# Convolution and gated MLP on one core: the second product sums its row halves in two banks side by side

## The chip, the cores and the metric

The kernel runs on one core of a Trainium2 chip. The metric is the device time of one execution in microseconds (us). Three runs of the kernel before took 718.79, 719.27 and 721.37 us; the median, 719.27, is what the change is measured against.

A core has five queues that run by themselves and wait for each other through semaphores: TensorE (PE, matmuls; its weight loads are listed apart as PEld), VectorE (DVE), ScalarE (ACT), GpSimd (POOL) and SyncE (SP), which computes nothing and issues transfers. Each works through its own instructions in the order in which the program gives them.

## The reference

The input x has 8 sequences of 4096 tokens with 192 channels in float32. There are two stages.

1. A causal convolution over 7 tokens. The channels fall into 8 heads of 24; each head has its own 7 weights, put through a softmax first: `out[b,s,h,:] = sum_k softmax(weight)[h,k] * x[b, s+k-6, h, :]`, with zeros ahead of the sequence.
2. A gated MLP on each of the 32768 tokens: `h = x @ w_in` (192 to 2048), `g = h * cos(h)`, `out = g @ w_out` (2048 to 192).

The kernel's matmuls take bf16 operands and sum in float32.

## The kernel before

**Tiles and units.** A tile (index t) is 512 tokens, and there are 64. A unit (index u) is two tiles: loading, casting, convolution and transposing go by units, both products by tiles. The main loop runs 66 times, since work on a tile trails its first product by up to two passes. A pass with even t is the first of its unit, one with odd t the second (`second`).

**Way of the data.** SP loads a unit of x; POOL casts it to bf16. PE convolves it by matmuls against a banded matrix (`conv_mm`), ACT copies the sums into ct (`conv_out`), and POOL doubles it (`double_unit`). SP then issues one transposing transfer for the unit (`turn_unit`), so that the channels come to lie on the partitions in cT, and POOL mends a few columns of it (`mend_edges`). Product 1 (`mm1`) multiplies cT with w_in in eight groups per tile. Each group fills two PSUM banks of h. For each, ACT makes cos(h) as a sine with an offset, and DVE multiplies h by it, which gives g (`gcu`). Product 2 (`mm2_step`) multiplies g with w_out into o_ps; a copy brings o_ps to SBUF (`evac`), and SP stores it (`store`).

**Row halves.** Nearly all matmuls use half of PE's rows: the upper 64 and the lower 64 work as two arrays at once, so matmuls come in pairs (r = 0 and r = 1). Each half sums over its part of the contraction, and both sums must end in the same bank. [...] They therefore take turns on two banks, and at each change of turns the half that comes to a bank waits until the other has left it. The class `Turn` does this through a no-op on SP's queue: `mark` makes the no-op wait for the last matmul of one half, and `wait` makes the first matmul of the other half wait for the no-op. Convolution parts take a turn in the same manner: c1 is the half of a part ahead of its turn, c2 the half after it.

**Product 2 before.** Work is cut into phases of 32 steps. In phase n the upper rows sum into one bank, and the lower rows sum into the bank that the upper rows filled in phase n - 1. So the two banks of a tile (b = 0 and 1, each for 256 of its tokens) come ready one phase apart, ACT copies both out, and there are 129 phases, of which the first and the last have one half only.

**PSUM.** Six of the eight banks are a ring of three buffers (`h_pool`), which product 1 and the convolution share; the other two hold o_ps.

**The orders.** Nothing is scheduled by a tool: strings give the order of the work on PE and ACT. In `PE_ORDER` (line 400, steady) h0 to h7 are the groups of product 1, c1 and c2 the convolution, m7 means seven steps of product 2 (a pair of matmuls each), and p and q mark places where a phase has ended. `ACT_ORDER` has s0 to s7 for the cosines (DVE's products go with them), ec1 and ec2 for the copies of the convolution, P and Q for the copies of o_ps. `PE_FIRST` and `ACT_FIRST` hold the first four passes. The transfers are tied to p and q: `turn_unit` for the next unit is issued at q of even passes, loads at p of odd passes, stores at p. SP's queue so holds loads, transposes, stores and the no-ops of the turns, in that order in which the loop writes them.

Of the kernel before, what the change touches and what calls it, by code (L numbers as in the profile page):

```python
# [8 lines left out]
FP32 = mybir.dt.float32  # L9
# [7 lines left out]
def kernel(  # L17
# [8 lines left out]
    nc = tc.nc  # L26
    B, S, D = x.shape
# [4 lines left out]
    T = 512  # L32
    NT = NTOK // T
    NB = T // 128
    U = 1024
    NU = NTOK // U
# [35 lines left out]
    def load_unit(u, n0=0, n1=UB, queue=nc.sync):  # L72
        if n0 == 0:
            x_tiles[u] = xin.tile([128, UB + 1, D], FP32, name="x_f")
        queue.dma_start(out=x_tiles[u][:, n0:n1, :],
                          in_=xf[u * U + n0 * 128 : u * U + n1 * 128, :].rearrange("(n p) d -> p n d", p=128))
# [119 lines left out]
    def conv_out(u, c, ps, n0, m0, m1, copy, double=False, banks=(0, 1)):  # L196

        for b in banks:
            w0 = (2 * c + b) * 2 * R
            o = ct_tiles[u][:, m0:m1, :, :, w0 : w0 + 2 * R].rearrange("p n k t w -> p (n k) t w")  # L200
            i = ps[b][:, (m0 - n0) * 2 * G : (m1 - n0) * 2 * G].rearrange("p (m t w) -> p m t w", t=1, w=2 * R)
            if double:
                copy(o, i.to_broadcast([128, (m1 - m0) * NC, 2, 2 * R]))  # L203
            else:
                copy(o[:, :, 0, :], i[:, :, 0, :])  # L205

    def ring_banks():
        h = h_pool.tile([128, 2, T], FP32, name="h")
        return [h[:, 0, :], h[:, 1, :]]
# [39 lines left out]
    def turn_unit(u, n0=0, n1=UB + 1):  # L249
        ct = ct_tiles.pop(u)  # L250
        if u not in cT:
            cT[u] = cT_pool.tile([128, UB + 1, NC, 128], BF16, name="cT")
        nc.sync.dma_start_transpose(out=cT[u][:, n0:n1].rearrange("p n c k -> p (n c) k"),
                                    in_=ct[:, n0:n1].rearrange("p n c t k -> p (n c t k)"))
        cT.pop(u - 2, None)
# [62 lines left out]
    def conv_rest():  # L318
        banks = o_banks()
        for c in range(2):  # L320
            for i in range(4):
                for prev in range(2):
                    conv_mm(0, c, [b[:, 4 * G * 2 * c :] for b in banks], i, slice(0, 128), NB + 1 - prev, UB + 1 - prev, prev,
                            start=c == 0 and prev == 0 and i % 2 == 0, stop=c == 1 and prev == 1 and i % 2 == 1)
        for b in range(2):
            for c in range(2):
                conv_out(0, c, [x[:, 4 * G * 2 * c :] for x in banks], NB, NB, UB, copies[1 - b], True, (b,))

    conv_first()
    turn_first(0)  # L330
# [31 lines left out]
    STEPS = 2 * NF  # L362

    def mm2_step(q):
        phase, i = divmod(q, STEPS)
        f, si = divmod(i, 2)
        for r in range(2):
            tt, b = divmod(phase - r, 2)
            if not 0 <= tt < NT:
                continue  # L370
            if r == 0 and i == 0:

                last = (tt, b) == (NT - 1, 1)
                o_ps[tt, b] = ring_banks()[0] if last else o_pools[b].tile([128, T], FP32, name="o_ps%d" % b)
            rows = slice(64 * r, 64 * r + 64)
            s = 2 * b + si
            m = nc.tensor.matmul(out=o_ps[tt, b][:, si * D : (si + 1) * D],  # L377
                                 lhsT=g_tiles[tt][rows, f, s * 128 : (s + 1) * 128], rhs=wo[rows, f // 2, f % 2, :],
                                 start=(r == 0 and i == 0), stop=(r == 1 and i == STEPS - 1), skip_group_check=True)
            if r == 0 and i == STEPS - 1:  # L380
                turns[tt, b] = Turn()
                turns[tt, b].mark(m)
            if r == 1 and i == 0:
                turns.pop((tt, b)).wait(m)

    def evac(t, b):
        if b == 0:
            o_sb[t] = opool.tile([128, NB, D], FP32, name="o_sb")
        nc.scalar.copy(o_sb[t][:, 2 * b : 2 * b + 2, :].rearrange("p s d -> p (s d)"), o_ps.pop((t, b))[:, 0 : 2 * D])  # L389

    def store(t, b0=0, b1=2):
        nc.sync.dma_start(out=out[t * T + b0 * 256 : t * T + b1 * 256, :].rearrange("(n p) d -> p n d", p=128),
                          in_=o_sb[t][:, 2 * b0 : 2 * b1, :])

    o_ps, o_sb, turns = {}, {}, {}
# [1 line left out]

    PE_ORDER = "h0 m7 c1 m6 c2 m4 h1 m7 q h2 h3 m12 h4 m10 h5 m10 h6 h7 p m8"  # L400
    ACT_ORDER = "s0 ec1 ec2 s1 Q s2 s3 s4 s5 P s6 s7"

    PE_FIRST = ["h0a h0b h1 h2 r h3 h4 h5 d1 d2 h6 h7 c1 c2 p",
                "m8 h0 m2 h1 m11 h2 m7 h3 m4 q h4 m9 d1 d2 m7 h5 m7 h6 m1 c1 c2 m8 p h7",
                "m9 c1 m1 h0 m6 c2 m9 h1 m7 q h2 h3 m15 h4 m5 h5 m12 p h6 h7",
                "m8 c1 m6 c2 m5 h0 m9 h1 m3 h2 m1 q h3 m14 h4 m7 h5 m11 h6 h7 p m8"]
    ACT_FIRST = ["s0a s0b s1 s2 s3 s4 s5 ed1 ed2 s6 ec1 ec2 s7", "s0 s1 s2 s3 s4 ed1 ed2 s5 s6 P ec1 ec2 s7",
                 "s0 ec1 ec2 s1 Q s2 s3 s4 s5 P s6 s7", "ec1 ec2 s0 s1 Q s2 s3 s4 s5 P s6 s7"]

    HALVES = {"": (0, NB), "a": (0, NB // 2), "b": (NB // 2, NB)}  # L410
    step = 0
    for t in range(NT + 2):
        u, second = divmod(t, TPU)
        cu, cc = (u + TPU, second) if t >= TPU else (1 + t, 1)
        conv = {"c": conv_part(cu, cc, ring_banks if t else o_banks, t < TPU) if cu < NU else iter(())}
        if t < TPU:
            conv["d"] = conv_part(cu, 0, ring_banks if t else o_banks, True)
        act, done, h = (ACT_ORDER if t >= len(ACT_FIRST) else ACT_FIRST[t]).split(), set(), {}

        def flush():  # L420
            while act:
                k = act[0]
                need = {"P": "p", "Q": "q", "e": k[1:2] + "2"}.get(k[0], "h" + k[1:])
                if need not in done:
                    return
                act.pop(0)
                if k == "P" and 0 <= t - 1 < NT:
                    evac(t - 1, 0)
                elif k == "Q" and 0 <= t - 2 < NT:
                    evac(t - 2, 1)  # L430
                elif k[0] == "e":
                    next(conv[k[1]], None)
                elif k[0] == "s" and t < NT:
                    gcu(t, int(k[1]), h.pop(k[1:]), *HALVES[k[2:]])

        for k in (PE_ORDER if t >= len(PE_FIRST) else PE_FIRST[t]).split():
            if k[0] == "h" and t < NT:
                h[k[1:]] = mm1(t, int(k[1]), *HALVES[k[2:]])
            elif k[0] in conv:
                next(conv[k[0]], None)  # L440
            elif k == "r":
                conv_rest()
                turn_unit(0, NB, UB)
                load_unit(2)
                load_edges(2)
                for q in range(2):
                    nc.gpsimd.tensor_copy(out=wo[:, q * HP : (q + 1) * HP], in_=wo_f[:, q * HP : (q + 1) * HP])  # L447
            elif k[0] == "m":
                for q in range(step, step + int(k[1:])):
                    mm2_step(q)  # L450
                step += int(k[1:])
            elif k[0] == "p":
                assert step % (2 * STEPS) == 0
            elif k[0] == "q":
                assert step % (2 * STEPS) == STEPS
            done.add(k)
            flush()

            if k == "q":
                if second == 0 and t and u + 1 < NU:  # L460
                    turn_unit(u + 1)
                    mend_edges(u + 1)
                if t == 1:
                    turn_unit(1)
                    cast_unit(3)
                    mend_edges(1)
                if second == 0 and u + 3 < NU:
                    cast_unit(u + 3)
                if second == 1 and t > 1 and cu < NU:
                    double_unit(cu)  # L470
                if t == NT + 1:
                    store(NT - 1, 1, 2)
            if k == "p":
                if t < NT + 1 and 0 <= t - 2:
                    store(t - 2)
                if t == NT:
                    store(NT - 1, 0, 1)
                if second == 1 and u + 4 < NU:
                    load_unit(u + 4)
                    load_edges(u + 4)  # L480
        if t == 0:
            double_unit(1)
            load_unit(3)
            load_edges(3)
            cast_unit(2)
        if t == 1:
            double_unit(2)
# [30 lines left out]
```

## Time and profile before

| what | value |
|---|---|
| span of the profiled execution | 717.4 us |
| PE busy | 707.9 us, 99% |
| ACT busy | 618.1 us, 86% |
| DVE busy | 611.5 us, 85% |
| POOL busy | 149.1 us, 21% |
| product 1 on PE (L347), one matmul | 376 ns as recorded |
| product 2 on PE (L377), one matmul | 243 ns as recorded |
| cosine on ACT (L354) | 1028 ns |
| g on DVE (L358) | 1219 ns |
| copy of o_ps on ACT (L389) | 473 ns |
| transfers | 85.24 MB, mean 119 GB/s |

Matmuls overlap in PE's pipeline, so the recorded duration of one isn't what it costs; the distance between starts is. In the lists of waits a row names who waited, for whom, for how many us in total, how many times, and the longest. Timeline rows give the start, the length, the engine, the line and the operation, with like neighbours merged (x12 is twelve instructions). A row of one line's instructions gives the count, then minimum, median and maximum duration in ns. A name such as SPq stands for an engine's queue itself: waiting and issuing, no computing.

### The profile page before, as it was taken

The numbers are of one execution on the slowest core, as the hardware profiler recorded it, in microseconds if no ns is written. First come the engines' busy times: TensorE is split into PE (matmuls) and PEld (weight loads), VectorE is DVE, ScalarE is ACT, GpSimd is POOL, SyncE is SP. The second block draws the span as 40 slices with busy tenths as digits, with TensorE's granted clock in tenths as the row PEclk, the third lists the DMA queues.
The fourth block names the chain that finished last, engine by engine and source line by source line (L and its number), as shares of the span: only waits on it lengthen the run. The fifth ranks groups of instructions, "written<-read, shape, count | busy, mean of one in ns | idle before, by whom it ended". The sixth has DMA issues, their size and how long they took to land.

```text
span 717.4 us, 26317 instructions
## 1 busy us (share of the span) xinstructions
PE 707.9 (99%) x11827; PEld 529.9 (74%) x11827; DVE 611.5 (85%) x536; ACT 618.1 (86%) x781; POOL 149.1 (21%) x123
## 2 busy tenths in 40 slices
PE   7999999999999999999999999999999999999997
PEld 3677777777777777777777777777777777777776
DVE  7788888888888888888888888888888888888984
ACT  7888888888888888888898888888888888888883
POOL 5622112221022221022220122220122221121000
PEclk9999999999999999999999999999999999999999
DMA  8945544445534356634355534566434455424312
GB/s 216 204 101 144 145 103 115 96 122 145 144 102 118 86 132 145 127 108 114 87 146 145 122 103 109 102 144 145 111 108 100 119 145 144 105 64 93 77 46 68
DMA packets 183664, 85.24 MB, mean 119 GB/s; under 512 B 111616, under 2 KB 183168, under 8 KB 183552
## 3 DMA queue, kind: packets, MB, share of 16 engines
q1 hardware_dynamic: 183128, 82.78, 47.6%
q8 instruction: 92, 1.51, 0.9%
q0 software_dynamic: 416, 0.79, 0.8%
q14 instruction: 20, 0.16, 0.1%
q10 hardware_dynamic: 8, 0.00, 0.0%
HBM read 31.36 MB, written 25.17 MB: 79 GB/s over the span
## 4 chain that ended last, share of the span: by engine, by line
PE 96%; ACT 1%; DVE 1%; DMA 1%; POOL 0%; issue 0%; DVEq 0%; POOLq 0%
PE o_ps L377 47%; PE h L347 46%; PE h L190 3%; DMA cT<-ct 1%; ACT cs L354 1%; PE h L377 0%; DVE g L358 0%; DVE band L279 0%; DVEq L513 0%; POOL mask L128 0%; ACT mask L133 0%; ACT ct L298 0%; DVE diag L269 0%; ACT ct L203 0%; DVE cT L316 0%
## 5 line engine op out<-in xcount | busy, mean ns | idle before, releaser
L358 DVE TENSOR_TENSOR g<-h,cs 128x1024 bf16<-128x1024 f32 (+1 forms) x513 | 603.4, 1217 | 92.3 <-ACT cs L354 87.4
L354 ACT ACTIVATE cs<-h 128x1024 bf16<-128x1024 f32 (+1 forms) x513 | 511.6, 1026 | 59.2 <-PE h L347 52.0
L377 PEld LDWEIGHTS <-g 64*128 64x128 bf16 x8192 | 362.2, 94 | 85.6 <-DVE g L358 0.8
L377 PE MATMUL o_ps<-wo,g 64*128 64x192 bf16 x8128 | 424.5, 243 | 1.0 <-DVE g L358 0.5
L347 PE MATMUL h<-cT,w 64*128 64x512 bf16 (+1 forms) x3078 | 399.1, 376 | 1.7 <-DVE g L358 0.9
L347 PEld LDWEIGHTS <-w 64*128 64x128 bf16 x3078 | 154.8, 94 | 87.2 <-issue 2.5
L259 POOL COPY cT<-cT 128x144 bf16<-128x144 bf16 x31 | 9.6, 309 | 495.4 <-DMA cT<-ct 409.1
L179 POOL CAST x_bf<-x_f 128x1728 bf16<-128x1728 f32 (+1 forms) x32 | 80.6, 2519 | 8.0 <-DMA x_f<-in_x_dram 7.8
L205 ACT CAST ct<-h 128x432 bf16<-128x432 f32 x120 | 56.4, 522 | 26.4 <-PE h L190 26.4
L389 ACT COPY o_sb<-o_ps 128x384 f32<-128x384 f32 x127 | 60.1, 473 | 4.8 <-PE o_ps L377 4.8
L247 POOL COPY ct<-ct 128x1728 bf16<-128x1728 bf16 x31 | 50.5, 1630 | 18.1 <-ACT ct L205 17.8
L190 PE MATMUL h<-x_bf,band 64*128 64x216 bf16 (+1 forms) x472 | 42.7, 254 | 0.0
L190 PEld LDWEIGHTS <-band 64*128 64x128 bf16 (+1 forms) x496 | 22.1, 94 | 4.4 <-issue 1.5
L105 PE MATMUL o_ps<-zero 128*128 128x512 bf16 x12 | 4.5, 536 | 1.3 <-DVE zero L100 1.3
L377 PE MATMUL h<-wo,g 64*128 64x192 bf16 x64 | 5.8, 243 | 0.0
L105 PEld LDWEIGHTS <-zero 128*128 128x128 bf16 x15 | 1.5, 118 | 3.2 <-issue 1.6
L447 POOL CAST wo<-wo_f 128x1536 bf16<-128x1536 f32 x2 | 3.0, 1479 | 2.1 <-DMA wo_f<-in_moe_w_out_dram 2.1
L190 PE MATMUL o_ps<-x_bf,band 128*128 128x96 bf16 (+1 forms) x24 | 1.9, 223 | 0.8 <-POOL x_bf L179 0.8
L389 ACT COPY o_sb<-h 128x384 f32<-128x384 f32 x1 | 0.5, 480 | 2.4 <-PE h L377 2.4
L115 ACT ACT_TABLE_LOAD x1 | 1.3, 1283 | 1.4 <-PEq L502 1.4
L292 PE MATMUL o_ps<-x_bf,band 128*128 128x48 bf16 x32 | 1.4, 183 | 0.9 <-ACT x_bf L179 0.5
L292 PEld LDWEIGHTS <-band 128*128 128x128 bf16 x32 | 1.2, 96 | 1.6 <-POOL band L279 1.6
(48 smaller groups left out, 29.6 us busy)
## 6 DMA issues: line engine op xcount, KB each, us to landing
out_dram<-o_sb SPq DMA_DIRECT2D x63, 384.0 KB
x_f<-in_x_dram SPq DMA_DIRECT2D x31, 768.0 KB
x_f<-in_x_dram SPq DMA_DIRECT2D x31, 96.0 KB
wo_f<-in_moe_w_out_dram SPq DMA_DIRECT2D x4, 384.0 KB
x_f<-in_x_dram SPq DMA_DIRECT2D x2, 384.0 KB
w<-in_moe_w_in_dram POOLq DMA_DIRECT2D x2, 384.0 KB, 6.2
cT<-ct SPq DMA_TRANSPOSE x32
out_dram<-o_sb SPq DMA_DIRECT2D x2, 192.0 KB
```

Of the source, the lines that this page charges most:

```text
L105: nc.tensor.matmul(out=bank, lhsT=zero[:, 0:128], rhs=zero, start=True, stop=True)
L179: copy(out=bf[u][:, n0 + o : n1 + o, :].rearrange("p n (h k r) -> p (n h) k r", k=NC, r=R), in_=x_tiles[u][:, n0:n1, :].rearrange("p n (h ...
L190: return nc.tensor.matmul(out=ps[i // 2][:, 0 : (n1 - n0) * 2 * G].rearrange("p (n k i r) -> p i n k r", n=n1 - n0, k=NC, i=2)[:, i % 2], ...
L205: copy(o[:, :, 0, :], i[:, :, 0, :])
L247: nc.gpsimd.tensor_copy(out=ct[:, n0:n1, :, 1, :], in_=ct[:, n0:n1, :, 0, :])
L259: nc.gpsimd.tensor_copy(out=cT[u][:, 0:UB, :, 0 : K - 1], in_=cT[u][:, UB].rearrange("p c (n t) -> p n c t", t=16)[:, :, :, 8 : 8 + K - 1])
L347: nc.tensor.matmul(out=h[:, i, n0 * 128 : n1 * 128], lhsT=w[rows, k, j, :], rhs=c[rows, m0 + n0 : m0 + n1, k, :], start=(k == 0), stop=(k ...
L354: nc.scalar.activation(out=cs[:, :, part], in_=h[:, :, part], func=AF.Sin, bias=math.pi / 2.0, scale=1.0)
L358: nc.vector.tensor_tensor(out=g_tiles[t][:, 2 * j : 2 * j + 2, part], in0=h[:, :, part], in1=cs[:, :, part], op=ALU.mult)
L377: m = nc.tensor.matmul(out=o_ps[tt, b][:, si * D : (si + 1) * D], lhsT=g_tiles[tt][rows, f, s * 128 : (s + 1) * 128], rhs=wo[rows, f // 2, ...
L389: nc.scalar.copy(o_sb[t][:, 2 * b : 2 * b + 2, :].rearrange("p s d -> p (s d)"), o_ps.pop((t, b))[:, 0 : 2 * D])
L447: nc.gpsimd.tensor_copy(out=wo[:, q * HP : (q + 1) * HP], in_=wo_f[:, q * HP : (q + 1) * HP])
```

## The change

Product 2 goes by tiles instead of by overlapping phases. For the first 32 steps of a tile the upper rows sum into bank 0 and the lower rows into bank 1; for the second 32 they change banks. Both banks of a tile are then ready at once, and ACT copies one while DVE copies the other. There is one turn per tile instead of two, and no phase has one half only. q now marks the change of banks within a tile, p the end of a tile. The orders for PE and ACT are written anew to fit, the first four passes included. Two of the transfers' places move with p and q: `double_unit` goes from q to p, and loads stay at p but for the first passes. `turn_unit` keeps its line under q. In the first pass the rest of unit 0's convolution (`conv_rest`) becomes a generator, so that its matmuls and copies have their own places in the orders. For the last tile both banks come from the ring, and its two stores go out on two queues.

```diff
     def mm2_step(q):
-        phase, i = divmod(q, STEPS)
-        f, si = divmod(i, 2)
+        tt, i = divmod(q, 2 * STEPS)
+        half, k = divmod(i, STEPS)
+        f, si = divmod(k, 2)
...
         for r in range(2):
-            tt, b = divmod(phase - r, 2)
...
+            b = half ^ r
             rows = slice(64 * r, 64 * r + 64)
             s = 2 * b + si
...
-            if r == 0 and i == STEPS - 1:
-                turns[tt, b] = Turn()
-                turns[tt, b].mark(m)
-            if r == 1 and i == 0:
-                turns.pop((tt, b)).wait(m)
+        if i == STEPS - 1:
+            turns[tt] = Turn()
+            turns[tt].mark(*ms)
+        if i == STEPS:
+            turns.pop(tt).wait(*ms)
...
-        nc.scalar.copy(o_sb[t][:, 2 * b : 2 * b + 2, :].rearrange("p s d -> p (s d)"), o_ps.pop((t, b))[:, 0 : 2 * D])
+        copies[b](o_sb[t][:, 2 * b : 2 * b + 2, :].rearrange("p s d -> p (s d)"), o_ps.pop((t, b))[:, 0 : 2 * D])
...
-    PE_ORDER = "h0 m7 c1 m6 c2 m4 h1 m7 q h2 h3 m12 h4 m10 h5 m10 h6 h7 p m8"
-    ACT_ORDER = "s0 ec1 ec2 s1 Q s2 s3 s4 s5 P s6 s7"
+    PE_ORDER = "h0 m1 c1 m6 c2 m4 h1 m10 h2 p h3 m10 h4 m9 h5 m9 h6 m4 q h7 m11"
+    ACT_ORDER = "s0 ec1 ec2 Q s1 P s2 s3 s4 s5 s6 s7"
...
-                need = {"P": "p", "Q": "q", "e": k[1:2] + "2"}.get(k[0], "h" + k[1:])
+                need = {"P": "p", "Q": "p", "e": "r" if k == "er" else k[1:2] + "2"}.get(k[0], "h" + k[1:])
...
+            if k == "p":
                 if second == 1 and t > 1 and cu < NU:
                     double_unit(cu)
+                if 0 <= t - 2 < NT - 1:
+                    store(t - 2)
                 if t == NT + 1:
                     store(NT - 1, 1, 2)
-            if k == "p":
-                if t < NT + 1 and 0 <= t - 2:
-                    store(t - 2)
-                if t == NT:
-                    store(NT - 1, 0, 1)
-                if second == 1 and u + 4 < NU:
-                    load_unit(u + 4)
-                    load_edges(u + 4)
+                    store(NT - 1, 0, 1, nc.scalar)
+            if k == ("p" if t > 1 else "q") and second == 1 and u + 4 < NU:
+                load_unit(u + 4)
+                load_edges(u + 4)
```

The new first four passes are left out here; they have no m in the first pass, as before, and 52, 50 and 69 steps in the next three (before: 64, 64 and 72).

## The prediction

> **What bounds the kernel now.** I read the busy shares first, then the tenths of the span, then the chain that ended last, then what TensorE waited for.
>
> ```profile
> PE 707.9 (99%) x11827; PEld 529.9 (74%) x11827; DVE 611.5 (85%) x536; ACT 618.1 (86%) x781; POOL 149.1 (21%) x123
> PE   7999999999999999999999999999999999999997
> PE 96%; ACT 1%; DVE 1%; DMA 1%; POOL 0%; issue 0%; DVEq 0%; POOLq 0%
> ```
>
> PE is busy in 99% of 717.4 us, only the two end slices fall below 9 tenths, and 96% of the chain is PE's own work. A busy PE alone isn't a proof; the list of PE's waits is:
>
> ```profile
> PE h L347 <- DVE g L358: 0.9, 3, 0.4
> PE o_ps L377 <- DVE g L358: 0.5, 1, 0.5
> ```
>
> Its rows, of which these are two (total us, times, longest us), add to under 6 us, nearly all in the first 23 us. In the steady part PE never waits: the kernel is as long as its matmuls. Their prices come from the timeline of PE in one tile:
>
> ```profile
> 305.26 0.81 PE L347 MATMUL h<-cT,w 64*128 64x512 bf16 x6
> 305.91 0.74 PE L377 MATMUL o_ps<-wo,g 64*128 64x192 bf16 x14
> 306.49 0.36 PE L190 MATMUL h<-x_bf,band 64*128 64x216 bf16 x4
> 306.67 0.67 PE L377 MATMUL o_ps<-wo,g 64*128 64x192 bf16 x12
> 307.17 0.36 PE L190 MATMUL h<-x_bf,band 64*128 64x216 bf16 x4
> ...
> 308.91 1.47 PE L347 MATMUL h<-cT,w 64*128 64x512 bf16 x12
> 310.20 1.17 PE L377 MATMUL o_ps<-wo,g 64*128 64x192 bf16 x24
> 311.19 0.61 PE L347 MATMUL h<-cT,w 64*128 64x512 bf16 x4
> ```
>
> Differences of starts give: an h group (6 matmuls) 305.91 - 305.26 = 0.65 us; 12 steps of product 2 (24 matmuls) 311.19 - 310.20 = 0.99, so 0.0825 a step; half a conv part (c1 or c2) 306.67 - 306.49 = 0.18. A tile is 8 x 0.65 + 64 x 0.0825 + 2 x 0.18 = 10.84 us, and tile starts stand 10.85 apart in the chain (59.58, 70.43, 81.28). There is no slack in PE.
>
> The last view is SP's own timeline, because the row halves take turns through no-ops on SP's queue:
>
> ```profile
> 298.42 4.70 SPq L253 DMA_TRANSPOSE cT<-ct  x1
> ...
> 320.11 4.08 SPq L253 DMA_TRANSPOSE cT<-ct  x1
> ```
>
> ```profile
> L253 SPq DMA_TRANSPOSE cT<-ct x32: 2617/4100/4898, 16.7 to 666.9; - x32
> ```
>
> Issuing one transpose holds SP for 4.1 us (minimum, median, maximum in ns; 2617 is the small first one; the full ones are 4.03 to 4.90). In the kernel before, the next no-op of SP executes 0.18 to 1.05 us after every steady transpose, since it belongs to the turn at p, 5.1 us later. So this hold costs nothing now, with little to spare.
>
> [...] So the 4.1 us are the queue's, not the transfer's. The trace agrees: behind the first transpose (16.69, 2.62 us long) the next load issues at 19.41, 0.10 us after its end, and no SP instruction overlaps another. [...] the trace has a granted clock of 1.00 throughout the steady part[...]. [...] the trace has a 128x384 PSUM copy on DVE (L316) at 558 ns, and I use 0.56.
>
> **The change part by part.**
>
> *Steps of product 2.* Before, phases overlap and the first and last carry one row half only: 129 x 32 = 4128 steps. After: 64 x 64 = 4096. A step with one half costs as much as one with two (32 in 2.83 us at the end), so 32 x 0.0825 = 2.6 us go. At most 8 of the 32, the m8 of the second tile, ran while PE then waited for a transpose to land (0.6 us wait at 22.1), so 24 are sure: 2.0 us. I take 2.0.
>
> *Evacuation.* ACT loses one 0.47 us copy per tile (L389), DVE gains one of 0.56. DVE has 85% of 10.85, so 9.3 us; with the copy 9.8 of 10.85. It fits. In time, from the start of a tile: h1 ends at 2.58, m10 ends at 3.40, and 0.3 us later the last sums are there (0.24 us matmul and the semaphore), so both copies start at 3.7 and end by 4.3. PE first needs the banks after h2 and h3, at 4.70. Margin 0.4: nothing is paid. DVE's g1 is queued behind the copy and starts at about 4.1, 0.2 later than it could; g2 can start at 5.3 only. The h ring has three buffers; walking it with 0.92 us per cosine and 1.14 per g back to back, PE's tightest ring wait keeps 0.07 us, no worse than before.
>
> *Turn inside a tile (q).* m4 q h7 m11: the sums must be seen by SP and back in the 0.65 us of h7. At 298.42 SP issued behind such a no-op 0.34 after q, so the no-op itself ran about 0.2 after it; back on PE 0.07 later (at the end: no-op 707.97, weight load 708.03). Hidden by h7, margin 0.38. Turns of product 2 halve, which saves nothing on PE.
>
> *The transpose and the conv turn.* Here the change moves a hold in front of a no-op. turn_unit stays at q of even tiles, but q was a third into the tile with 5 us to the next no-op, and now stands near its end. Behind it in SP's queue comes the no-op of the next tile's c1, and c2's weight loads wait for that. PE from q to c2: h7 0.65 + m11 0.91 + h0 0.65 + m1 0.08 + c1 0.18 + m6 0.50 = 2.97 us. SP from q: 0.34 until the transpose issues, H = 4.09 hold (the common value), 0.13 to the no-op and back to PE: 4.56. PE stands 4.56 - 2.97 = 1.6 us with m4, h1 and all else queued behind c2. It can't be made up on an engine without slack. It happens after the transposes of tiles 2, 4, ... 58, whose next tile has a conv part: 29 times. 29 x 1.6 = 46 us. Bounds: H = 4.03 gives 1.5 and 44; H = 4.9 each time gives 2.4 and 70; the mean of the steady ones before (4.25) gives 51. The long ones (4.7 and up) may come of the input load still moving, which now issues 4.7 us ahead (293.73); after, the load (at p of the odd tile) is some 16 us ahead, so I take the common 4.09.
>
> *Rest.* Landing of the transpose: 6.9 us after issue as now (298.4 to the mend at 305.3), so some 5.7 us into the odd tile, with over 5 us before its reader: hidden. conv_rest one h later in tile 0: its DVE copies (15.59) wait for DVE anyway. The tail: two 192 KB stores together instead of one, about 1 us more, against one lone turn of 0.3 us less and a late g (0.5 us wait at 707.4) that is no longer met: zero.
>
> Sum: 719.3 - 2.0 + 46.2 = 763.5 us.
>
> **The rivals.**
> *A, no hold in the way:* the no-op passes, or the hold shrinks below 2.5 us in its new place. For it: PE then has only less work. Against it: no full transpose under 4.03. Time: 719.3 - 2.0 = 717.3, or 716.6 with all 32 steps: no slower, within 0.5%.
> *B, the hold meets other traffic:* holds of 4.7 to 4.9 throughout, or thin ring margins break and DVE pays another 0.3 us per tile. For it: seven of the thirty steady ones were long. Against: loads have moved away. Time: 717.3 + 29 x 2.4 = 787; or 763.5 + 62 x 0.3 = 782.
> *C, the clock falls* in the 1.6 us gaps[...].
>
> **How the numbers follow.** Forecast 0.82, A 0.10, B 0.06, C 0.02. The forecast's own range is H from 4.03 to 4.5 and 0.2 us per gap for the parts of the walk: 29 x 1.3 to 29 x 2.0, so 755 to 775. Outside of it lie A, C, B's larger times and little of the forecast, together 0.2. Slower by over 0.5% (3.6 us) is forecast, B and C: 0.88 with a little off for A's edge cases. A is a gain of 2 to 2.7 us, mostly within 0.5%: same 0.09, faster 0.03.
>
> **What would show it.** Right: PEld L190 waits for SP's no-op of L164 about 29 times, 1.5 to 1.7 us each; chain starts of odd and even tiles 10.85 and 12.4 apart; c2 starting about 0.13 us after each transpose's end; PE's share about 93%; no wait of product 2 for either copy; fewer matmul steps at both ends. Wrong: no such waits (A); waits of 2.4 us or of h on g in each tile (B); a granted clock below 1.00 (C). The forecast fails if the hold depends on where the transpose stands or if the no-op need not wait its turn.

## The result and the profile after

The changed kernel takes 774.69 us (median; 772.27 to 779.56), against 719.03 for the kernel before: ratio 1.0776, 95% interval 1.0719 to 1.0833. It is slower, by 55.7 us where 44.2 was forecast.

Busy shares and chain of the changed kernel, in the profiled execution. It is the slowest of the four, 779.56 us, and its span is 777.9:

```profile
PE 717.1 (92%) x11826; PEld 518.2 (67%) x11827; DVE 647.4 (83%) x600; ACT 603.2 (78%) x717; POOL 147.7 (19%) x123
PE 78%; SPq 17%; issue 2%; ACT 1%; DMA 1%; DVE 1%; POOL 1%; POOLq 0%
```

SP's queue, which computes nothing and was no part of the chain before, now holds 17% of it. (That counts whole holds of SP, not only the part that PE waited for.) What PE waited for (total us, times, longest):

```profile
PE h L190 <- SPq L164: 47.0, 29, 2.2
PE h L349 <- POOL cT L259: 2.5, 1, 2.5
```

There are 29 waits for the turn's no-op, as many as forecast. No row of PE's waits names o_sb: product 2 waits for neither copy. One gap in full, first from SP's timeline, then from PE's:

```profile
310.72 4.09 SPq L253 DMA_TRANSPOSE cT<-ct  x1
```

```profile
312.68 0.35 PE L190 MATMUL h<-x_bf,band 64*128 64x216 bf16 x4
312.86 0.66 PE L382 MATMUL o_ps<-wo,g 64*128 64x192 bf16 x12
314.93 0.36 PE L190 MATMUL h<-x_bf,band 64*128 64x216 bf16 x4 [1.41 <-SPq L164]
```

The six steps from 312.86 take 0.50 us, so c2 could start at 313.36. The transpose holds SP until 314.81, and c2 starts at 314.93, 0.12 later: a gap of 1.57 us. The wait in the bracket, 1.41, is shorter than the gap because the matmuls as recorded reach over their issue: the row of twelve ends at 313.52, 0.16 behind 313.36. By starts (the distance between two starts, less 0.08 for the step itself), the 29 gaps are 1.53 to 2.32 us, mean 1.78, median 1.62, together 51.6 us. The holds behind them:

```profile
L253 SPq DMA_TRANSPOSE cT<-ct x32: 2778/4131/4840, 16.8 to 733.5; - x32
```

The other 8.9 us of the 60.5 by which the spans differ lie in two places. In the start, the third pass waits for the mended columns of unit 1:

```profile
31.10 4.11 SPq L253 DMA_TRANSPOSE cT<-ct  x1
...
37.21 0.31 POOL L259 COPY cT<-cT 128x144 bf16<-128x144 bf16 x1 [5.97 <-DMA cT<-ct]
...
37.57 0.82 PE L349 MATMUL h<-cT,w 64*128 64x512 bf16 x6 [2.55 <-POOL cT L259]
```

Before, this transpose was issued at 27.02, since q stood earlier in the second pass. And in some places the granted clock falls (busy time of each engine, then PEclk, the DMA share and GB/s):

```profile
218.00:220.00 2.00, 0.76 (x16) 0.65 (x18) 0.67 (x1) 0.36 (x1) 0.00 (x0) 1.00 1.27 289
...
221.00:222.00 1.00, 1.00 (x16) 0.97 (x14) 0.00 (x0) 0.99 (x1) 0.00 (x0) 0.50 0.00 0
222.00:223.00 1.00, 1.00 (x12) 0.65 (x10) 0.40 (x1) 0.40 (x2) 0.96 (x2) 0.50 0.00 0
```

After the gap at 217 to 219.2 PE runs at half speed for 3.41 us. The profiled execution has five such windows ahead of its last microseconds: one at 22.07, in a wait of the start, and four right behind gaps of 2.1 to 2.3 us, at 52.80, 148.37, 220.05 and 619.41. From each start to the next it is 9, 28, 21 and 117 times 3.413 us, so in this trace the windows start on a fixed grid. The gaps that cost one fit it: of the eight gaps over 2.1 us, the four that a window follows have 2.15 us or more inside one stretch of the grid, and the other four are cut by its bounds, with at most 1.64 us in one stretch. A gap of 2.01 us in one stretch brought none.

One pass with a window takes 14.7 us where 12.4 + 0.7 for its longer hold would do: about 1.6 us per window. The four timed executions have mean clocks of 0.998, 0.995, 0.995 and 0.988 in the order of their times, 772.27, 774.59, 774.80 and 779.56. What PE loses by it is about 1.5, 3.9, 3.9 and 9.3 us (estimates: span times one minus the mean clock), so the clock can account for their spread of 7.3.

Sum for the profiled one: 51.6 of gaps + 5 x 1.6 of clock + 2.5 in the start - 2.0 for the steps saved = 60.1 us, of 60.5. The 2.0 in it is the forecast's, not measured here.

### The profile page after: what moved, and what is told of

Read it like the earlier page. It is cut to its first block, busy times and chain, and to the rows that moved or that the text cites. A ratio compares the mean times of both kernels' runs of the same rounds, so it can differ in the third digit from the quotient of the medians.

```text
span 777.9 us, 26315 instructions
## 1 busy us (share of the span) xinstructions
PE 717.1 (92%) x11826; PEld 518.2 (67%) x11827; DVE 647.4 (83%) x600; ACT 603.2 (78%) x717; POOL 147.7 (19%) x123
## 4 chain that ended last, share of the span: by engine, by line
PE 78%; SPq 17%; issue 2%; ACT 1%; DMA 1%; DVE 1%; POOL 1%; POOLq 0%
PE h L349 37%; PE o_ps L382 37%; SPq L253 16%; PE h L190 3%; DMA x_f<-in_x_dram 1%; PE h L382 1%; ACT cs L356 0%; POOL x_bf L179 0%; DVE g L360 0%; DVE band L279 0%; SPq L164 0%; ACT ct L205 0%; POOL mask L128 0%; SPq L69 0%; SPq L75 0%
## 5 line engine op out<-in xcount | busy, mean ns | idle before, releaser
L382 PEld LDWEIGHTS <-g 64*128 64x128 bf16 x8192 | 356.3, 95 | 100.0 <-issue 3.2
L349 PE MATMUL h<-cT,w 64*128 64x512 bf16 (+1 forms) x3078 | 410.2, 379 | 5.7 <-POOL cT L259 2.5
L349 PEld LDWEIGHTS <-w 64*128 64x128 bf16 x3078 | 144.9, 95 | 85.5 <-issue 6.7
L394 DVE COPY o_sb<-o_ps 128x384 f32<-128x384 f32 x63 | 35.1, 557 | 83.6 <-PE o_ps L382 83.2
L394 ACT COPY o_sb<-o_ps 128x384 f32<-128x384 f32 x63 | 29.9, 474 | 3.5 <-PE o_ps L382 3.5
```

Source lines behind the costliest of these rows:

```text
L349: nc.tensor.matmul(out=h[:, i, n0 * 128 : n1 * 128], lhsT=w[rows, k, j, :], rhs=c[rows, m0 + n0 : m0 + n1, k, :], start=(k == 0), stop=(k ...
L382: ms.append(nc.tensor.matmul(out=o_ps[tt, b][:, si * D : (si + 1) * D], lhsT=g_tiles[tt][rows, f, s * 128 : (s + 1) * 128], rhs=wo[rows, f ...
L394: copies[b](o_sb[t][:, 2 * b : 2 * b + 2, :].rearrange("p s d -> p (s d)"), o_ps.pop((t, b))[:, 0 : 2 * D])
```

## Experiments

The theory: SP's hold by the transpose stands between c1 and c2 of the next pass. The rivals: product 2 waits for its two banks and DVE's copy; or the transfer and not the hold hurts.

**1. The hold moved out of the way.** The transpose goes behind c2's turn of the same pass.

```diff
-            if k == "q":
+            if k == "c2":
                 if second == 0 and t and u + 1 < NU:
                     turn_unit(u + 1)
                     mend_edges(u + 1)
+            if k == "q":
```

> The changed kernel, with the transpose of even passes issued right after c2 of the same pass instead of at q. Theory (the hold of SP stands between c1 and c2 of the next pass): SP is held some 1.3 to 6 us into the pass, where no turn waits, so the 29 gaps (51.6 us in the trace of after) go and nothing else changes: 720 us, 718 to 722, with what the start lost still in it. Rival 1 (both banks ready at once, or DVE's copy, cost the time): stays above 760. Rival 2 (the new place makes the turn at q late): waits of product 2 for SP, 725 to 740.

Measured: 719.83 us; against the kernel before 1.0011, 1.0004 to 1.0017. The transpose still holds SP as long, and PE's rows are those of the start (its longest three):

```profile
298.28 4.17 SPq L253 DMA_TRANSPOSE cT<-ct  x1
302.55 9.89 SPq L397 DMA_DIRECT2D out_dram<-o_sb  x2
```

```profile
PE h L349 <- POOL cT L259: 2.5, 1, 2.5
PE h L349 <- DMA cT<-ct: 1.6, 1, 1.6
PE o_ps L105 <- DVE zero L100: 1.3, 1, 1.3
```

So 54.9 of the 55.7 us hang on where one transfer per unit is issued. Between 40 and 700 us PE waits for nothing, though DVE is now busy 90%. The rival of banks and copies falls, since both are as in the changed kernel. The same bytes are moved, but at another time; experiment 3 leaves them where they were.

**2. The same loss made in the kernel before.** The same edit in the old kernel, with "p" for "c2".

> The kernel before, with nothing changed but the transpose of even passes issued at p instead of at q. Theory: SP takes the transpose up 0.34 us after the steps ahead of h6 end and reaches the no-op of the next c1 4.56 to 4.7 us after them; PE reaches c2 after h6 h7 (1.30), m8 (0.66), h0 (0.65), m7 (0.58), c1 (0.18), m6 (0.50) = 3.87. So 29 gaps of 0.7 to 0.9 us: 719 + 20 to 26 = 739 to 745. Rival (the hold hurts only through what the change did to banks and copies): 719, no waits for SP.

Measured: 764.14 us, ratio 1.0627 (1.0612 to 1.0642); 29 gaps, together 42.5 us, median 1.27. The rival falls, since nothing of the change is in it. But the size was missed: 42.5 us of gaps, where 20 to 26 were expected. SP's and PE's timelines show why:

```profile
321.32 4.18 SPq L253 DMA_TRANSPOSE cT<-ct  x1
325.61 8.32 SPq L392 DMA_DIRECT2D out_dram<-o_sb  x2
```

```profile
326.24 0.36 PE L190 MATMUL h<-x_bf,band 64*128 64x216 bf16 x4 [1.19 <-SPq L164]
```

At p a store stands between the transpose and the no-op. Its issue at 325.61 takes 0.52 us (the row merges it with the next store), and with the steps between SP's instructions the no-op comes about 0.6 us later. 0.7 + 0.6 = 1.3. So the 0.52 us of the store counted here beside the 4.18 of the transpose. The profiled execution took 761.5, which is 719 + 42.5; the 2.6 us to the median lie in the other three executions, whose mean clocks are 0.994 to 0.998 against 1.000. By the same estimate that is 1.5 to 4.6 us, so the clock can account for them. In the profiled one, with a mean clock of 1.000, no window follows any gap, though one is 2.5 us long.

**3. No turn in the convolution.**

```diff
-        conv = {"c": conv_part(cu, cc, ring_banks if t else o_banks, t < TPU) if cu < NU else iter(())}
+        conv = {"c": conv_part(cu, cc, ring_banks if t else o_banks, True) if cu < NU else iter(())}
```

> The changed kernel, with every convolution part done by matmuls over all 128 rows (4 instead of 8, the same time on PE), so that no convolution part takes a turn; transposes stay where the change put them. Theory: no no-op stands behind the hold until the turn at q 12 us later, so the gaps go; two switches between halves and whole rows per part cost about 0.25 us by the second pass of before, 60 parts, 15 us: 735, 725 to 742. Rival (the transpose's transfer itself or the traffic slows PE): above 765.

Measured: 732.94 us. The transposes stay at q and PE doesn't wait for SP, so the transfer by itself is not what costs the 55 us. Against the first experiment 13.1 us more are paid, 0.22 us for each of 60 parts. I put them down to the change between half and whole rows; no run tries that alone.

**4. PE reaches c2 later.**

```diff
-    PE_ORDER = "h0 m1 c1 m6 c2 m4 h1 m10 h2 p h3 m10 h4 m9 h5 m9 h6 m4 q h7 m11"
+    PE_ORDER = "h0 m7 c1 m6 c2 m1 h1 m7 h2 p h3 m10 h4 m9 h5 m9 h6 m4 q h7 m11"
```

> The changed kernel, with six steps of product 2 moved from after c2 to before c1 in the steady order (m7 c1 m6 c2 m1 h1 m7 instead of m1 c1 m6 c2 m4 h1 m10). Theory: PE reaches c2 0.50 us later while SP is held, so each of 28 or 29 gaps shrinks from 1.78 to 1.28 us: 14 us less than the changed kernel in a run without low clock, 758, 754 to 763. Rival (the gap isn't set by SP's time): same as the changed kernel, 772 to 775.

Measured: 759.83 us, 14.9 less than the changed kernel. The gaps have a median of 1.13 instead of 1.62, which is 0.49 for six steps of 0.0825 = 0.50, and sum to 39.3, 12.3 less. The rest goes with the clock, 0.998 to 1.000 here against 0.988 to 0.998: in the profiled execution no window follows these gaps.

**5. The rest: unit 1's transpose early.** On top of the first experiment, after h3 of the second pass:

```diff
+            if t == 1 and k == "h3":
+                turn_unit(1)
+                cast_unit(3)
+                mend_edges(1)
...
-                if t == 1:
-                    turn_unit(1)
-                    cast_unit(3)
-                    mend_edges(1)
```

> The kernel of the first experiment, and unit 1's transpose, with its cast and its mending, issued after h3 of the second pass instead of at q. SP has nothing ahead of it, so it goes out when unit 1 is doubled, at about 24 us instead of 31. Theory (the rest of the forecast gain is lost in the start: 2.5 us wait of h0 of the third pass for the mended columns, and a half-speed window of 3.4 us in its wake, 1.7 us): 719.8 - 2.5 - 1.7 = 715.6, 715 to 718. Rival (the steady tile of the change is no cheaper and the start isn't it): 719.5 to 720.

Measured: 716.30 us, ratio to the kernel before 0.9966 (0.9953 to 0.9978): faster than both kernels, by 2.5 us against the one before (718.81 in the same series). The wait of h0 for the mended columns is 0.2 us instead of 2.5:

```profile
PE h L349 <- DMA cT<-ct: 2.0, 1, 2.0
...
PE h L349 <- POOL cT L259: 0.2, 1, 0.2
```

The half-speed window that the first experiment's profile has at 36 us is gone as well: from 24 to 40 us the granted clock is 1.00, where it was 0.89. The size is that of the 32 saved steps (2.0 to 2.6), but the profiles don't show it as theirs. From the start of the fifth pass to that of the 63rd, where no step is saved, PE takes 627.4 us against 628.4 before: a tile is 10.83 us long, where it was 10.83 and 10.86 in turn. Why stays open. And the fifth pass starts at 56.28 us in the profiled execution, the slowest of this experiment (718.09), and at 55.34 in experiment 6, against 55.74 before, though 29 steps (2.4 us) fewer are done by then. So about 1 us comes from the steady tiles, and the new start gives back part of what the steps save.

**6. Steps into the wait of the start.** On top of the fifth, the second pass begins with "p m8 h0 m1 h1 m3 h2 m6 h3 m1 h4 m1 h5 m12 q".

> The kernel of the run before, and eight steps of product 2 moved to the start of the second pass, ahead of h0, where PE waits for the first transpose to land (1.6 us). Theory: eight steps of 0.0825 run in that wait: 0.7 us less than the run before, 715 to 717. Rival (VectorE's work sets the pace of the first two passes, so steps moved ahead leave a hole later): the same as the run before within 0.3 us.

Measured: 717.17 us (717.02 to 718.38), 0.9 us longer than the fifth, whose executions reach from 716.05 to 718.09. Both numbers were missed. PE's wait for the transpose goes, but others come in its place:

```profile
PE h L349 <- DVE g L360: 1.6, 6, 0.4
PE o_ps L382 <- ACT ct L205: 1.3, 2, 1.1
```

That is what the rival expected: steps moved ahead leave a hole later, for DVE and a copy.

**7. Both copies on ACT.** On top of the first experiment; in the steady order, and likewise in the fourth pass:

```diff
-        copies[b](o_sb[t][:, 2 * b : 2 * b + 2, :].rearrange("p s d -> p (s d)"), o_ps.pop((t, b))[:, 0 : 2 * D])
+        nc.scalar.copy(o_sb[t][:, 2 * b : 2 * b + 2, :].rearrange("p s d -> p (s d)"), o_ps.pop((t, b))[:, 0 : 2 * D])
...
-    ACT_ORDER = "s0 ec1 ec2 Q s1 P s2 s3 s4 s5 s6 s7"
+    ACT_ORDER = "s0 ec1 ec2 s1 Q P s2 s3 s4 s5 s6 s7"
```

> The kernel of the first experiment, with both copies of o_ps on ACT (after s1, one behind the other) and none on DVE. By the walk of the prediction: the copies start 3.7 us into the tile, the second ends at 4.5 to 4.6, PE needs the bank at 4.70. Theory (evacuation by two engines isn't needed for the banks to be free in time): 719.8, within 0.5. Rival (the second engine is what makes the side by side banks work): PE waits for the copies, 0.3 us or more in each of 62 tiles, 738 or more.

Measured: 720.04 us, the same as the first (719.83), with no wait of PE between 40 and 700 us. Evacuation by two engines is worth nothing measurable here: h2 and h3 hide two copies in a row.

**8. The hold twice.** In the changed kernel a second transpose, into a tile that nobody reads, follows each one from unit 2 on.

```diff
+        if u > 1:
+            again = spare_pool.tile([128, UB + 1, NC, 128], BF16, name="spare")
+            nc.sync.dma_start_transpose(out=again[:, n0:n1].rearrange("p n c k -> p (n c) k"),
+                                        in_=ct[:, n0:n1].rearrange("p n c t k -> p (n c t k)"))
```

> The changed kernel, with a second transpose of the same unit, into a spare tile that nobody reads, issued behind each one from unit 2 on: the suspected cost doubled. Theory: 29 gaps grow from 1.8 by one hold to about 6 us: 772 + 29 x 4.2 = 894 from SP's time alone; [...] 915 to 950. Rival 1 (no clock effect of the gaps): 890 to 897. Rival 2 (SP can run ahead of a second transfer): 772 to 780.

Measured: 964.30 us. The 29 gaps grow from 51.6 to 176.4 us, by 4.30 each, which is one hold. The spans differ by 184.7, so 60 us more are lost than the gaps show. That is over the 915 to 950 expected. Its row of the granted clock, and PE's wait (lines stand one further down in this kernel):

```profile
PEclk9988899889998889988899888998889888899899
...
PE h L191 <- SPq L165: 171.7, 29, 6.5
```

After each of the 29 gaps (5.75 to 6.65 us) the clock is at half for 6.8 us, in five cases for 3.4, part of it in the gap itself; the mean clock is 0.906. With the changed kernel's own windows (8 us), which these replace, 68 us or 2.3 us per gap go to the clock. The range allowed 1.7, half of one window of 3.41 us as in the changed kernel's trace (estimate): 894 + 29 x 1.7 = 943.

**9. Half of the hold at q.** Four blocks at q, five after c2 of the odd pass.

```diff
-        ct = ct_tiles.pop(u)
+        ct = ct_tiles[u] if n0 == 0 and n1 < UB + 1 else ct_tiles.pop(u)
...
+            if k == "c2" and second == 1 and t > 1 and u + 1 < NU:
+                turn_unit(u + 1, NB, UB + 1)
+                mend_edges(u + 1)
             if k == "q":
                 if second == 0 and t and u + 1 < NU:
-                    turn_unit(u + 1)
-                    mend_edges(u + 1)
+                    turn_unit(u + 1, 0, NB)
```

> The changed kernel, with the transpose in two parts: four of the nine blocks at q of even passes, the other five after c2 of the odd pass, behind the turn. The work of the transposes is the same, and a transpose still stands at q. Theory (only the part of a hold that outlasts PE's 2.97 us from q to c2 costs): the hold at q is 12/27 of 4.1 = 1.8 us (the first transpose, of 12 of 27, took 2.6 with the start's traffic), SP is back at 0.34 + 1.8 + 0.13 = 2.3, up to 3.1, so no gap, or 0.1: 720, 719 to 723. Rival (a transpose at q costs whatever its length, by its transfer or a fixed part): 740 or more.

Measured: 720.25 us, as the first, and none of PE's longest waits is for SP. The part at q cost nothing measurable: with its median hold of 1.46 us SP is back 0.34 + 1.46 + 0.13 = 1.9 us after q (estimate from the measured parts), and PE reaches c2 at 2.97 (the row has both parts):

```profile
L253 SPq DMA_TRANSPOSE cT<-ct x62: 1302/1556/4079, 16.7 to 676.1; - x62
```

## Why the prediction was right, and where its sizes were off

*PE has no slack; gaps can't be made up.* Right: in experiment 4 the time follows the gaps, in experiment 8 the gaps and the clock.

*Steps of product 2, 2.0 us.* Not shown by itself. Experiment 5 gains 2.5 us, but about 1 of it lies in the steady tiles, where no step is saved. The prediction put the halved turns there at nothing; whether they are the cause stays open.

*Evacuation, nothing paid.* Right. DVE's copy takes 557 ns, and experiment 7 shows that even one engine would do.

*Turn at q, hidden by h7.* Right: in the steady part of the first experiment no step waits for it.

*The turns.* That the halves need them is not shown: no run leaves one out where two halves sum into one bank.

*The transpose and the conv turn.* Mechanism and count (29) right, and 0.13 us from SP back to PE was measured as 0.12. The term that was too small is the gap: 1.6 forecast, 1.78 on average. Long holds stayed (up to 4.84, from 639.98), though the loads ahead were issued 15 us earlier, at 624.21 and 624.75, so their nearness isn't what makes them long; what does is not shown. The median gap is the forecast 1.6, but a sum follows the mean: the mean hold is 4.28 and not 4.09. The term's upper working (mean of before, 4.25, 51 us) is what came: 51.6. That is 5.4 us of the miss.

*Rest, zero.* Failed. I looked at conv_rest and at the tail, but not at the first full transpose, which also hangs on q: from 27.0 to 31.1 us, and 2.5 us of waiting. The tail was right: from the start of the last h group to the end 13.6 us before (703.11 + 0.65 to 717.4) and 13.3 after (764.53 to 777.85).

*Rival C.* I took it as all or nothing, at 0.02; no trace that I had shows how long a gap must be, so that was a guess. It came in part: a window of 3.41 us at half speed followed four of the eight gaps over 2.1 us, and none of the shorter ones; 2.15 us of idling inside one stretch of 3.413 was enough. From its mean clock of 0.995, about two such windows are in the median execution, some 3 us (estimate).

Together: 763.5 + 5.4 + 2.5 + 3 = 774.4, of 774.7.

*The range, 755 to 775.* The mechanism, the count and the median gap were right. That the median execution lies inside, by 0.3 us, is in part luck: the range was made for errors of the gap alone, and the start and the clock came on top; the slowest execution, 779.56, lies outside. The sum of the range also has a slip: its lower end takes 0.2 us per gap for the parts of the walk, its upper end leaves them out and would have been 781 with them.

## What to carry to other kernels

Here the no-op on SP's queue came only after the issues ahead of it: a transpose of 4.09 us in the changed kernel, one of 4.18 and a store of 0.52 in experiment 2. Before moving a place in the order to which transfers are tied, list what follows each long issue on its queue and who waits for that. The 32 holds (medians 4.10 and 4.13 us) stood in no engine's busy share, in the kernel before as in the changed one, where they showed up as PE's 29 waits and 17% of the chain. So read the queue's own timeline. And where a saving of 0.4% is at stake, the first three passes deserve the same walk as the steady one.

## What the runs showed of the hardware

Issuing a whole transpose took more here than issuing it in two parts. A unit's nine blocks of tokens have 27 blocks of 128 columns; parts of 12 and 15 of these held SP for 1.46 and 1.60 us (medians in experiment 9), a whole one for 4.1 (median in the kernels before and after). Two parts held it 3.1 us together, a quarter less; by the means, 3.4 against 4.3, it is a fifth. I have not tried why.

In the changed kernel's trace the half-speed windows of PE's clock start on a grid of 3.413 us. In the steady part, gaps with 2.15 us or more inside one stretch of it brought a window; none came after 2.01 us in one stretch, or after gaps of up to 2.32 us that a bound of the grid cuts with at most 1.64 on one side. In experiment 2 none came after a gap of 2.5 us; where it lies on such a grid is not shown. The gaps of experiment 8, 5.75 to 6.65 us, brought half speed each time, for 6.8 or 3.4 us.
